# A second buffer for k, an earlier load of one batch's k, half a transpose on TensorE, and a new order on VectorE in a hand-scheduled attention and MLP kernel

## The chip, the cores and the metric

One core of one Trainium2 chip. The metric is the device time of one execution in microseconds (us). Before the change the median was 270.38 us over the first three runs (270.26 to 271.22).

In the profile, PE is TensorE, PEld its weight loads, DVE is VectorE, ACT is ScalarE, POOL is GpSimd, SP is SyncE and SPq its queue, from which most DMA transfers are issued. In a timeline each line is: start, length, engine, source line, operation, output<-inputs, shape, number of instructions; in brackets the idle time ahead of it and what ended that. Source lines of an experiment are shifted by one to three, as it adds lines to the tables at the top.

## The reference, cut to what matters

```python
# q, k, v: 8 batches x 8 heads x 576 x 64, float32
q_s = softmax(q, axis=-1)             # over the 64 features
k_s = softmax(k, axis=2)              # over the 576 positions
kv  = einsum('bhsd,bhse->bhde', k_s, v)
x   = einsum('bhsd,bhde->bhse', q_s, kv)      # -> 4608 tokens x 512
h   = x @ w_in                                # 512 -> 2048
out = (h * sigmoid(h)) @ w_out                # 2048 -> 512
```

## The kernel before

The tokens go through in nine chunks (0 to 8). Each has a first product (x with w_in, then silu on ScalarE) and a second product (with w_out). Chunks 3 to 8 do both products by a seven-product scheme (Winograd's form of Strassen) instead of eight; the chunks before lead into that: chunk 0 is all standard, chunk 1 has a standard first product and a seven-product second one, chunk 2 does half of its first product in each way. Beside that run the attention of the batches ahead: exps, row sums, normalisation, the transpose of q, kv, and the product of q with kv that makes the next chunk's input (called the input product here, or xt).

The kernel fixes the order of each engine's instructions itself: they stand in the order in which they were recorded. That order comes from tables of positions, one per chunk; all pieces are sorted by position and then recorded:

```python
def mid(b):                       # attention of batch b, placed in chunk b-1
    p = PLAN[b - 1]
    for i in range(4):            # two exps of q, two of k
        x, y = (("qt", "eq"), ("kt", "ek"))[i // 2]
        put(b - 1, p["ex"][i], exp, b, x, y, i % 2)
    for cc in range(2):
        put(b - 1, p["qs"][cc], qsum, b, cc)                       # DVE row sum
        put(b - 1, p["qn"][cc], qnorm, b, cc, ENG[p["qe"][cc]])    # DVE or POOL
        # ... vcast, kv, kvcopy (cut)
    # loads of the batch after, from SP's queue
    put(b - 1, p["lq"], load, b + 1, "qt", q)
    put(b - 1, p["lk"], load, b + 1, "kt", k)
    put(b - 1, p["lv"], load, b + 1, "vt", v)
    if "tt" in p:                 # part of the transpose on TensorE
        if len(p["th"]) == 1:
            put(b - 1, p["tp"], tr_dma, b, nc.sync, 1 - p["th"][0])
        # ... tr (nine transposes) and trc (copy from PSUM) (cut)
    else:
        put(b - 1, p["tp"], tr_dma, b, nc.sync)    # all of it by one DMA transfer
```

The buffers, and the copy (the *ring* is the set of six PSUM tiles that the first product fills in turn; s1, u2 and the like are the sums that turn the seven products into the result, XS those of the input):

```python
LDB = {"qt": 1, "kt": 1, "vt": 1}     # SBUF buffers of loaded q, k, v
PSB = {"ring": 6, "ops": 2}           # PSUM: tiles of the first product, banks of the second

def after(t, k):                      # what follows product k of chunk t's second product
    ...
    if k == 1:                        # s1: the first PSUM bank copied out
        if PLAN[t + 1]["m1"][0]:
            nc.vector.tensor_scalar_mul(out=new("s1"), in0=o, scalar1=c)
        else:
            nc.scalar.activation(out=new("s1"), in_=o, func=ACT.Copy, scale=c)
    elif k == 6:
        add(new("u2"), WP[t, "s1"])   # DVE, reads the other bank
```

The softmax here doesn't subtract the row's maximum and nothing guards it: scores larger than these inputs give would overflow.

Of the kernel before, what the change touches and what calls it, by code (L numbers as in the profile page):

```python
# [16 lines left out]
WARM = 1  # L17

PLAN = {
    0: {'y': [31.0, 33.0, 33.0, 33.5, 34.0, 34.5, 35.0, 35.0, 36.5, 37.0, 39.5, 41.5, 42.5, 44.5, 46.0, 47.0], 'ex': [31.7, 34.3, 38.3, 39.4], 'qs': [32, 36.0], 'qn': [36.5, 37.0], 'vs': [40.5, 37.5, 44.5, 44.0], 'ks': [45.0, 45.3], 'kc': [45.51, 46.81], 'lq': 33.5, 'tp': 38.0, 'ox': [47.1, 47.7], 'oc': [47.11, 47.71], 've': [2, 0, 1, 2], 'order': [(1, 0), (2, 0), (3, 1), (3, 0), (0, 0), (0, 1), (1, 1), (6, 0), (2, 1), (5, 0), (6, 1), (7, 1), (4, 0), (11, 0), (8, 1), (5, 1), (4, 1), (7, 0), (8, 0), (9, 0), (9, 1), (11, 1), (10, 1), (13, 1), (12, 1), (14, 0), (14, 1), (10, 0), (15, 0), (12, 0), (15, 1), (13, 0)], 'ke': [1, 0], 'oe': [0, 1], 'qe': [0, 0], 'pad': 16, 'th': [0, 1], 'tt': [42.5, 37.4, 43.0, 40.4], 'tc': [43.51, 40.5, 43.01, 42.5], 'te': [0, 2, 0, 0]},  # L20
    1: {'ex': [15.7, 17.22, 23.74, 21.26], 'qs': [17.5, 19.0], 'qn': [19.51, 19.1], 'vs': [25.0, 20.0], 'ks': [26.0, 21.5], 'kc': [26.51, 25.01], 'lq': 17.0, 'lk': 20.6, 'lv': 23.2, 'tp': 20.5, 'ox': [28.0, 28.5], 'oc': [29.01, 28.51], 've': [2, 2], 'pa': [11.4, 13.0, 11.5], 'pae': [0, 0, 0], 'ke': [1, 1], 'oe': [2, 1], 'std': 4, 'order': [], 'add': {}, 'act': {}, 's1': {0: 0, 1: 0, 2: 0, 3: 1}, 'sl': [1.5, 1.5, 3.0, 6.0, 5.0, 9.5, 6.5, 9.0, 10.0, 11.5, 12.5, 11.0, 14.5, 13.0, 15.0, 15.0], 'xs': [6.8, -21.4, -1.0, -4.5], 'xe': [0, 0, 1, 1], 'pad': 14, 'qe': [1, 0]},
    2: {'std': 2, 'order': [(3, 1), (3, 6), (2, 1), (2, 6), (3, 7), (3, 5), (2, 7), (3, 4), (2, 2), (2, 5), (3, 2), (2, 4), (2, 3), (3, 3)], 'y': [-13.0, -12.5, -11.0, -11.0, -11.0, -11.0, -10.0, -9.5, -8.0, -7.0, -3.5, -2.5, -2.0, -1.0], 'ex': [-1.207, -2.202, -1.08, 2.294], 'qs': [6.9, 1.4], 'qn': [11.91, 3.41], 'vs': [-1.58, 13.9], 'ks': [19.4, 19.9], 'kc': [19.41, 19.91], 'lq': 17.45, 'lk': 16.262, 'lv': 24.41, 'tp': 15.9, 'ox': [19.9, 20.4], 'oc': [19.91, 20.41], 'sl': [5.0, 5.5, 3.0, 4.0, 4.5, 7.5, 9.5, 10.0], 'add': {(3, 6): 9.55, (3, 3): 22.02, (3, 2): 16.02, (3, 1): 9.55, (2, 6): 11.55, (2, 2): 17.02, (3, 5): 13.55}, 'act': {(2, 3): 21.55, (3, 5): 17.02, (3, 3): 22.02, (2, 5): 19.02, (3, 4): 18.55, (2, 2): 16.02, (2, 1): 10.55, (2, 6): 15.02, (2, 4): 21.55, (3, 6): 9.55, (2, 7): 14.55}, 's1': {2: 0, 3: 1}, 'xs': [0.1, 2.1, 9.1, 2.6], 'pa': [19.95, 19.95, 20.45], 'ya': {5: -5.0, 4: -1.55, 2: -8.0, 7: -8.55, 3: -0.55}, 'm1': [0, 0], 'pb': [-14.9, -14.3, -14.2, -15.0, -10.5], 'xe': [0, 0, 0, 0], 'pae': [1, 1, 1], 'pbe': [0, 0, 0, 0, 0], 've': [1, 2], 'ke': [0, 1], 'oe': [1, 0], 'qe': [1, 0]},
}
STEADY = {'std': 0, 'order': [(0, 1), (0, 6), (0, 5), (0, 7), (0, 2), (1, 1), (0, 4), (1, 6), (0, 3), (2, 1), (1, 2), (1, 7), (1, 5), (2, 6), (1, 4), (1, 3), (2, 2), (2, 7), (2, 5), (2, 4), (3, 1), (3, 6), (2, 3), (3, 2), (3, 7), (3, 5), (3, 4), (3, 3)], 'y': [0.5, 1.5, 5.0, 6.0, 9.0, 9.5, 9.5, 12.5, 14.5, 18.0, 19.5, 22.5, 25.7, 28.402], 'ex': [3.798, 1.41, 3.92, 1.297], 'qs': [11.4, 6.9], 'qn': [12.41, 9.91], 'vs': [10.9, 12.92], 'ks': [19.4, 19.4], 'kc': [21.91, 20.41], 'lq': 8.95, 'lk': 23.9, 'lv': 24.41, 'tp': 17.4, 'ox': [23.4, 23.4], 'oc': [24.41, 26.41], 'sl': [], 'add': {(3, 6): 22.02, (0, 3): 8.02, (0, 2): 6.02, (0, 5): 5.02, (2, 2): 20.02, (1, 3): 15.55, (1, 4): 15.55, (2, 7): 17.55, (1, 2): 10.55, (0, 4): 8.02, (1, 1): 6.02, (2, 6): 14.55, (1, 6): 10.55, (3, 1): 20.55, (1, 7): 11.55, (3, 2): 24.02}, 'act': {(0, 2): 4.55, (0, 3): 10.02, (2, 5): 18.55, (0, 4): 9.02, (1, 5): 15.02, (3, 3): 27.404, (1, 3): 18.02, (0, 5): 5.02, (3, 4): 26.55, (1, 4): 17.02, (2, 4): 23.02, (2, 3): 23.02, (0, 6): 4.02, (1, 1): 8.02, (3, 6): 22.55, (0, 1): 2.55, (3, 5): 27.55, (2, 1): 13.02, (3, 2): 23.55, (3, 7): 27.02, (1, 7): 13.55, (2, 6): 15.02, (2, 7): 17.02, (1, 2): 12.55}, 's1': {0: 0, 1: 1, 2: 0, 3: 0}, 'xs': [0.296, 0.298, -0.227, 0.4], 'pa': [19.95, 27.407, 27.41], 'pb': [1.45, 1.96, 4.45, 4.46, 3.45], 'ya': {6: 8.0, 5: 18.5, 4: 22.95, 3: 28.852, 7: 14.5}, 'm1': [0, 0], 'xe': [0, 0, 1, 1], 'pae': [1, 1, 1], 'pbe': [0, 0, 1, 1, 1], 've': [1, 2], 'ke': [1, 1], 'oe': [0, 0], 'qe': [1, 1]}
for _t in range(3, 8):
    PLAN[_t] = STEADY
PLAN[8] = {'std': 0, 'order': [(0, 1), (0, 6), (0, 2), (0, 7), (1, 1), (0, 5), (0, 4), (0, 3), (1, 6), (1, 2), (1, 7), (1, 5), (1, 4), (2, 1), (1, 3), (2, 6), (2, 2), (2, 7), (2, 5), (3, 1), (2, 4), (2, 3), (3, 6), (3, 2), (3, 7), (3, 5), (3, 4), (3, 3)], 'y': [1.5, 2.0, 5.5, 8.5, 10.0, 11.0, 14.0, 15.0, 19.0, 22.0, 24.5, 25.8, 27.401, 27.406], 'sl': [], 'add': {(2, 7): 17.55, (3, 2): 24.02, (3, 7): 24.55, (3, 4): 26.55, (3, 1): 20.55, (2, 3): 22.55, (0, 2): 3.55, (0, 3): 8.02, (2, 4): 20.55, (1, 4): 13.55}, 'act': {(2, 1): 15.55, (3, 6): 24.02, (3, 4): 26.55, (2, 3): 24.55, (2, 4): 21.55, (1, 7): 14.02, (2, 6): 19.02, (0, 3): 10.02, (1, 5): 12.55, (0, 4): 8.02, (3, 5): 27.403, (1, 4): 15.02, (2, 7): 21.02, (3, 7): 25.55, (1, 6): 10.02, (1, 3): 15.55, (3, 2): 23.55, (2, 2): 19.02, (3, 1): 20.02, (0, 5): 7.55, (1, 1): 6.55, (2, 5): 20.02}, 's1': {0: 1, 1: 0, 2: 1, 3: 1}, 'xs': [-0.71, -0.208, -0.207, 1.4], 'pa': [24.45, 27.45, 29.429], 'pb': [0.793, 3.96, 12.45, 10.46, 11.45], 'ya': {6: 10.0, 4: 27.401, 7: 15.45, 2: 11.95}, 'm1': [0, 0], 'xe': [0, 0, 1, 0], 'pae': [1, 1, 1], 'pbe': [0, 1, 0, 1, 0]}
PLAN[9] = {'y': [0, 1, 2, 3, 4, 5, 6, 7, 8, 9, 10, 11, 12, 13], 'ya': {}, 'm1': [0, 0], 'pb': [-0.201, -0.2, -0.2, 1.9, 2.9], 'pbe': [0, 0, 0, 0, 0]}
TXAT = [(0, (1, -39.0, 0, 1)), (0, (1, -12.0, 1, 1)), (1, (1, -39.0, 0, 1)), (1, (1, 4.0, 1, 1)), (2, (1, 2.5, 0, 0)), (2, (1, -15.0, 1, 1)), (3, (1, -1.0, 0, 1)), (3, (2, -18.0, 1, 1))]
TWAT = [(1, -11.0, 0), (1, 4.0, 0), (1, 5.5, 1), (1, 13.0, 1), (1, 13.0, 0), (1, 20.0, 0), (0, 37.0, 0), (0, 40.5, 0)]  # L30
WORDER = ['w10', 'w11', 'w12', 'w13', 'w20', 'q', 'w21', 'w22', 'k', 'w23', 'v0', 'v1']
GATE = ('ek', 0)
HV = (1, 1.5, 1)
JS = 5
STD = 0
START = {'qn': (0, 0), 'h': [4, 3, 2, 1], 'v': 0, 't': (0, 0, 0, 2), 'x': 1, 'o': 0, 'w': 4}
# [2 lines left out]
def kernel(  # L39
# [57 lines left out]
    ctx.enter_context(tc.manual_schedule())  # L97

    st = [dict() for _ in range(B)]
    LDB = {"qt": 1, "kt": 1, "vt": 1}  # L100

    def load(b, name, src, ccs=None, eng=nc.sync, js=(0, J)):
        if name not in st[b]:
            st[b][name] = ld.tile([128, NG, J * D], FP32, name=name, bufs=LDB[name])
        x = src[b].rearrange("(g r) (p j) d -> g (r p) (j d)", r=2, j=J).rearrange("g x y -> x g y")
# [127 lines left out]
    def xtcopy(t, cc, dve=0):  # L233
        for i, (off, size) in enumerate(part[t]):
            o1 = XO.pop((t, cc, i), None)
            if o1 is None:
                continue
            for g in range(2):
                x = XT[t][:, 2 * cc + g, off:off + size]
                if g < dve:  # L240
                    nc.vector.tensor_copy(x, o1[g][:, 0:size])
                else:
                    nc.scalar.copy(out=x, in_=o1[g][:, 0:size])
# [332 lines left out]
    def load_w(name):  # L576
        if name[:2] == "w1":
            f = slice(*WCUT[int(name[2])])
            nc.gpsimd.dma_start(
                out=W1[:, :, f], in_=w_in[:, f].rearrange("(c p) f -> p c f", p=128)  # L580
            )
        elif name[:2] == "w2":
            i = int(name[2])
            nc.gpsimd.dma_start(
                out=W2[:, i * 4:(i + 1) * 4, :],
                in_=w_out[i * 512:(i + 1) * 512, :].rearrange("(fc p) o -> p fc o", p=128),
            )
        else:
            cc = int(name[1]) if len(name) > 1 else None
            load(1, name[0] + "t", {"q": q, "k": k, "v": v}[name[0]], cc, eng=nc.gpsimd)  # L590
# [18 lines left out]
    nc.gpsimd.tensor_copy(gate[:, 0:1], gx)  # L609
    for name in WORDER[:START["w"]]:  # L610
        load_w(name)
# [32 lines left out]
    xtcopy(0, 1, 1)  # L644
    for name in WORDER[SB["w"]:]:
        load_w(name)
# [9 lines left out]
    def put(t, pos, f, *args):  # L656
        todo.append((base[t] + pos, len(todo), f, args))
# [3 lines left out]
    def load_first(b):  # L661
        st[b]["qt"] = ld.tile([128, NG, J * D], FP32, name="qt", bufs=LDB["qt"])
        V.tensor_copy(st[b]["qt"][0:1, 0, 0:1], vaug[0:1, J - 1, D:E1])
        for x in (("qt", q), ("kt", k), ("vt", v)):
            load(b, *x)
# [33 lines left out]
    def xtpair(t):  # L699
        p = PLAN[t - 1]  # L700
        for cc in range(2):
            put(t - 1, p["ox"][cc], xt, t, cc)
            put(t - 1, p["oc"][cc], xtcopy, t, cc, p["oe"][cc])
# [19 lines left out]
    if STD == 1:  # L723
        put(*HV[:2], halve, ENG[HV[2]])
    for i, x in enumerate(PLAN[0]["y"]):
# [11 lines left out]
    for t in range(1, NCH):  # L737
        xtpair(t)
    for i, x in TXAT:
        put(*x[:2], vsum, i, *((0, HF // 2), (HF // 2, HF))[x[2]], ENG[x[3]])  # L740
    for i, x in enumerate(TWAT):
        put(*x[:2], wsum, i // 2, i % 2, ENG[x[2]])
# [42 lines left out]
```

## Time and profile before

| what | before |
|---|---|
| median of all four runs | 270.32 us (269.69 to 271.22) |
| profiled run | 269.08 us, span of the core 267.2 us |
| PE busy | 254.0 us of the span |
| chunk 1's second product starts | 60.69 us |
| chunk 2's first matmul | 76.50 us |
| chunk 2's first Winograd product | 85.63 us |
| input products of chunks 4 and 8 | 116.93 and 221.26 us |

The rows with a time are start times, and they are the best ruler here. A matmul's end is modelled, and a wait can hide in it; a start can't. I call the distance from 60.69 to 85.63, 24.94 us, the *lead-in*, and that from 116.93 to 221.26, 104.33 us, the *steady stretch*.

### The profile page before, as it was taken

To read this page: it belongs to the slowest core of one execution; us is meant where nothing else is said; L and a number is where in the kernel's file an instruction comes from. 1 tells how busy PE (TensorE), PEld (TensorE's weight loads), DVE (VectorE), ACT (ScalarE), POOL (GpSimd) and SP (SyncE) were. 2 spreads that over 40 slices of the span, in tenths; PEclk is the share of its full clock that TensorE was granted. 3 is DMA by queue.
4 is the path that set the end of the run, shared out by engine and by line. 5 is a ranking of instruction groups with operands and counts; after the bars stand their busy time and mean duration, and the time that the engine had idled before them with its cause. 6 is when DMAs were issued, how large, how long until landed. Compare 5 with 4: busy or idle time off the path is not lost.

```text
span 267.2 us, 6566 instructions
## 1 busy us (share of the span) xinstructions
PE 254.0 (95%) x2686; PEld 199.4 (75%) x2686; DVE 192.4 (72%) x332; ACT 187.3 (70%) x327; POOL 150.1 (56%) x94
## 2 busy tenths in 40 slices
PE   8889999998997999999999999999999999999993
PEld 3468645456844778888888888888888887888882
DVE  2930088757785989969986889688967678898842
ACT  5789964769649799878987798779875457454300
POOL 2655903941104959794978496859685546603500
PEclk9999999999999999999999999999999999999999
DMA  7999999910996895459655955592631102110334
GB/s 257 324 205 273 245 337 394 322 30 11 248 287 234 199 398 183 107 122 355 218 111 106 360 179 120 110 328 76 128 82 43 39 22 59 42 39 9 77 76 118
DMA packets 40717, 45.90 MB, mean 172 GB/s; under 512 B 16368, under 2 KB 28656, under 8 KB 40688
## 3 DMA queue, kind: packets, MB, share of 16 engines
q1 hardware_dynamic: 35392, 37.63, 47.0%
q0 software_dynamic: 5136, 7.73, 12.9%
q8 instruction: 21, 0.34, 0.5%
q10 hardware_dynamic: 160, 0.13, 0.2%
q14 instruction: 8, 0.07, 0.1%
HBM read 36.70 MB, written 9.44 MB: 173 GB/s over the span
## 4 chain that ended last, share of the span: by engine, by line
PE 65%; DMA 9%; DVE 9%; ACT 8%; SPq 5%; issue 3%; DVEq 0%; ACTq 0%
PE ops L450 26%; PE hps L349 20%; PE hps L256 10%; DMA kt<-in_k_dram 7%; PE ops L535 5%; SPq L524 4%; DVE u L367 2%; ACT eq L118 2%; ACT GT L286 2%; DVE zq L137 1%; PE kvps L183 1%; DMA qt<-in_q_dram 1%; ACT ek L118 1%; PE o L225 1%; SPq L159 1%
## 5 line engine op out<-in xcount | busy, mean ns | idle before, releaser
L450 PEld LDWEIGHTS <-GT 128*128 128x128 bf16 x512 | 49.6, 98 | 7.5 <-issue 1.2
L349 PEld LDWEIGHTS <-TX 128*128 128x128 bf16 x416 | 40.2, 98 | 8.5 <-issue 3.1
L349 PE MATMUL hps<-XS,TX 128*128 128x256 bf16 x312 | 43.1, 273 | 1.7 <-DVE u L367 0.9
L367 DVE SCALAR_TENSOR_TENSOR u<-hps,u 128x512 f32<-128x512 f32 x52 | 35.8, 688 | 10.8 <-PE hps L349 8.4
L367 DVE SCALAR_TENSOR_TENSOR u<-hps,s 128x512 f32<-128x512 f32 x52 | 35.5, 683 | 9.7 <-PE hps L349 9.4
L450 PEld LDWEIGHTS <-SW 128*128 128x128 bf16 x384 | 37.3, 98 | 4.9 <-DVE SW L407 0.4
L137 DVE TENSOR_REDUCE zq<-eq 128x18 f32<-128x1152 bf16 x16 | 21.5, 1347 | 23.9 <-ACT eq L118 23.9
L256 PE MATMUL hps<-XT,W 128*128 128x320 bf16 (+3 forms) x224 | 35.7, 318 | 2.8 <-ACT GT L286 1.7
L391 ACT ACTIVATE GT<-u 128x512 bf16<-128x512 f32 x52 | 32.2, 630 | 6.7 <-DVE u L367 6.7
L256 PEld LDWEIGHTS <-W 128*128 128x128 bf16 x224 | 21.7, 98 | 16.5 <-issue 3.9
L349 PEld LDWEIGHTS <-W 128*128 128x128 bf16 x312 | 30.4, 98 | 4.1 <-issue 0.4
L450 PE MATMUL ops<-W,GT 128*128 128x256 bf16 x256 | 31.7, 273 | 1.1 <-ACT s L480 1.1
L450 PE MATMUL ops<-TW,SW 128*128 128x256 bf16 x256 | 32.7, 273 | 0.0
L450 PE MATMUL ops<-TW,GT 128*128 128x256 bf16 x256 | 32.6, 273 | 0.0
L349 PE MATMUL hps<-XT,W 128*128 128x256 bf16 x208 | 30.4, 273 | 0.0
L405 POOL TENSOR_TENSOR SW<-GT 128x1024 bf16<-128x1024 bf16 x7 | 14.9, 2130 | 26.9 <-ACT GT L391 16.8
L411 POOL TENSOR_TENSOR SW<-GT,SW 128x1024 bf16<-128x1024 bf16 x11 | 23.6, 2148 | 9.2 <-DVE SW L407 9.2
L286 ACT ACTIVATE GT<-hps 128x192 bf16<-128x192 f32 (+4 forms) x72 | 25.0, 418 | 4.4 <-PE hps L256 3.1
L145 POOL TENSOR_TENSOR eq<-eq,rzq 128x1152 bf16<-128x1152 bf16 x10 | 21.3, 2127 | 9.5 <-DVE rzq L138 9.5
L118 ACT ACTIVATE ek<-kt 128x1152 bf16<-128x1152 f32 x16 | 18.3, 1158 | 10.4 <-DMA kt<-in_k_dram 10.4
L409 POOL TENSOR_TENSOR GT<-GT 128x1024 bf16<-128x1024 bf16 x12 | 25.6, 2131 | 0.0
L391 ACT ACTIVATE GT<-s 128x512 bf16<-128x512 f32 x26 | 16.5, 633 | 9.9 <-DVE s L367 9.9
(78 smaller groups left out, 396.5 us busy)
## 6 DMA issues: line engine op xcount, KB each, us to landing
qt<-in_q_dram SPq DMA_DIRECT2D x6, 1152.0 KB, 5.7
kt<-in_k_dram SPq DMA_DIRECT2D x6, 1152.0 KB, 6.5
vt<-in_v_dram SPq DMA_DIRECT2D x6, 1152.0 KB, 8.2
out_dram<-u SPq DMA_DIRECT2D x34, 64.0 KB, 3.4
W<-in_moe_w_in_dram POOLq DMA_DIRECT2D x4, 512.0 KB, 8.6
W<-in_moe_w_out_dram POOLq DMA_DIRECT2D x4, 512.0 KB, 18.9
out_dram<-u SPq DMA_DIRECT2D x14, 128.0 KB, 2.7
qt<-in_q_dram SPq DMA_DIRECT2D x2, 576.0 KB, 4.2
```

Source lines behind the costliest of these rows:

```text
L118: nc.scalar.activation(out=o, in_=jgd(st[b][src], cc)[:, js], func=ACT.Exp)
L137: nc.vector.reduce_sum(out=st[b]["zq"][:, cc, js], in_=e, axis=AX.X)
L145: eng.tensor_tensor(out=e, in0=e, in1=r[:, :, :, None].to_broadcast([128, n, 2, D]), op=ALU.mult)
L256: nc.tensor.matmul(out=hps[:, 0:size], lhsT=W1[:, c, fb * 128:(fb + 1) * 128], rhs=XT[t][:, c, off:off + size], start=(c == 0), stop=(c == ...
L286: nc.scalar.activation(out=y, in_=hps[:, h], func=ACT.Silu)
L349: nc.tensor.matmul(out=o[:, f, :], lhsT=l(c, 2 * g + f), rhs=r(c), start=bool(first and f == 0 and c == 0), stop=(c == HK - 1), skip_group ...
L367: nc.vector.scalar_tensor_tensor(out=out, in0=o, scalar=1.0, in1=x, op0=ALU.mult, op1=ALU.add)
L391: nc.scalar.activation(out=y, in_=MP[t, g, x], func=ACT.Silu)
L405: V.tensor_add(S1[:, f], quad(t, 0, f, 1), quad(t, 1, f, 1))
L409: V.tensor_sub(quad(t, 0, f, 1), quad(t, 0, f, 0), quad(t, 0, f, 1))
L411: V.tensor_sub(S4[:, f], quad(t, 1, f, 0), S2[:, f])
L450: nc.tensor.matmul(out=o, lhsT=l(f), rhs=r(f), start=bool(first and (own or a == 0) and f == 0), stop=(f == HF - 1), skip_group_check=True,)
```

## The change

Its intent: remove TensorE's waits in the lead-in. Batch 3's k is loaded earlier, into a second buffer. Half of batch 2's q is transposed by TensorE, so that less hangs on the DMA transfer. The copy of the first bank goes to VectorE, which gets a new order around it. Chunk 0 is reordered to suit, with the first half of v loaded ahead of the last quarter of w_out, and batch 2's q later.

The diff, cut to its core (the tables of chunks 0 to 2 are almost wholly new; only entries that the text uses are kept, `...` marks cuts):

```diff
 PLAN = {
-    0: {... 'lq': 33.5, ...}
+    0: {... 'lq': 39.0, ...}
-    1: {'ex': [15.7, 17.22, 23.74, 21.26], 'qs': [17.5, 19.0], 'qn': [19.51, 19.1], ... 'lk': 20.6, ... 'tp': 20.5, ... 'oe': [2, 1], ...}
+    1: {'ex': [16.7, 16.72, 22.24, 23.26], 'qs': [17.65, 17.9], 'qn': [19.1, 18.1], ... 'lk': 7.5, ... 'tp': 18.1, ... 'oe': [0, 2], ... 'th': [0], 'tt': [22.5, 21.1], 'tc': [23.51, 24.6], 'te': [2, 2]}
-    2: {... 'ex': [-1.207, -2.202, -1.08, 2.294], ... 'm1': [0, 0], ... 'qe': [1, 0]}
+    2: {... 'ex': [0.2, -0.79, -3.6, -4.09], ... 'm1': [1, 0], ... 'qe': [1, 1]}
 }
-TXAT = [(0, (1, -39.0, 0, 1)), (0, (1, -12.0, 1, 1)), ...]
+TXAT = [(0, (0, -5.5, 0, 0)), (0, (0, 20.0, 1, 1)), ...]
-WORDER = ['w10', ..., 'w22', 'k', 'w23', 'v0', 'v1']
+WORDER = ['w10', ..., 'w22', 'k', 'v0', 'w23', 'v1']
-    LDB = {"qt": 1, "kt": 1, "vt": 1}
+    LDB = {"qt": 1, "kt": 2, "vt": 1}
```

## The prediction

> **What bounds the kernel now.** I read the busy table first, then the busy time by stretches, then TensorE's instructions in order of time wherever it sat idle, and last what the engine named as releaser was doing just before.
>
> The first two lines of the page and the row of the idle tail:
>
> ```profile
> span 267.2 us, 6566 instructions
> PE 254.0 (95%) x2686; PEld 199.4 (75%) x2686; DVE 192.4 (72%) x332; ACT 187.3 (70%) x327; POOL 150.1 (56%) x94
> PEclk9999999999999999999999999999999999999999
> ```
>
> TensorE is busy 95% at full granted clock. Whatever leaves its work alone can win only what it idles, 267.2 - 254.0 = 13 us. The busy times by stretch (columns: stretch, its length, then busy us of PE, PEld, DVE, ACT, POOL) tell where that idle time is:
>
> ```profile
> 0.00:15.70 15.70, 12.75 (x140) 5.81 (x140) 10.01 (x23) 9.38 (x12) 7.86 (x17) 1.00 0.94 277
> ...
> 60.70:76.30 15.60, 14.32 (x201) 11.56 (x199) 11.67 (x20) 12.21 (x18) 2.12 (x1) 1.00 0.62 144
> 76.30:85.60 9.30, 7.21 (x32) 3.14 (x33) 6.97 (x12) 6.58 (x9) 2.15 (x2) 1.00 0.87 317
> 85.60:97.00 11.40, 10.60 (x163) 8.28 (x162) 9.36 (x20) 9.56 (x20) 9.10 (x6) 1.00 0.82 243
> 97.00:141.00 44.00, 44.00 (x544) 38.82 (x543) 38.03 (x66) 38.16 (x60) 35.19 (x20) 1.00 0.67 198
> ...
> 260.00:267.20 7.20, 2.93 (x27) 2.38 (x25) 1.54 (x3) 0.00 (x0) 0.00 (x0) 1.00 0.44 109
> ```
>
> The start (3.0 us idle) and the tail (4.3 us) are not touched by the change. From 97 us on, the idle time is near zero until the tail. What is left, about 4.2 us, lies between 60.7 and 97 us: chunk 1's second product, chunk 2's first. TensorE's instructions there, in order of time (start, length, what; in brackets the idle time and who ended it):
>
> ```profile
> 62.44 1.99 PE L450 MATMUL ops<-TW,SW 128*128 128x256 bf16 x16
> 65.50 1.91 PE L450 MATMUL ops<-W,GT 128*128 128x256 bf16 x16 [1.07 <-ACT s L480]
> ...
> 75.05 1.05 PE L450 MATMUL ops<-W,SW 128*128 128x256 bf16 x8
> 76.50 0.39 PE L256 MATMUL hps<-XT,W 128*128 128x512 bf16 x1 [0.40 <-DVE XT L241]
> 77.09 5.12 PE L256 MATMUL hps<-XT,W 128*128 128x512 bf16 x23 [0.20 <-DVE XT L241]
> 83.91 1.89 PE L256 MATMUL hps<-XT,W 128*128 128x512 bf16 x8 [1.70 <-ACT GT L286]
> ```
>
> Modelled matmul ends hide some waiting, so I go by starts. A group of sixteen takes 1.75 us (60.69 to 62.44), so the start at 65.50 is 1.31 late; 76.50 and 77.09 are .58 and .37 late; 23 matmuls at .2185 from 77.09 end at 82.12, so 83.91 is 1.79 late. With .28 for three changes to small matmuls, that is 4.33 us lost from 60.69 to 85.63. ScalarE's instructions in the same time show why:
>
> ```profile
> 61.45 1.28 ACT L118 ACT_TABLE_LOAD   x1
> 62.75 2.22 ACT L118 ACTIVATE eq<-qt 128x1152 bf16<-128x1152 f32 x2
> 64.87 0.58 ACT L480 ACTIVATE s<-ops 128x512 f32<-128x512 f32 x1
> ...
> 79.73 2.22 ACT L118 ACTIVATE ek<-kt 128x1152 bf16<-128x1152 f32 x2 [2.69 <-DMA kt<-in_k_dram]
> 81.97 1.28 ACT L286 ACT_TABLE_LOAD   x1
> ```
>
> The copy of the first bank stands behind a table load and two exps, and TensorE needs that bank again. Later ScalarE itself idles 2.69 us for batch 3's k, issued at 72.66 because the only k buffer was being read until then. The two exps and the table load come after it, so the first silu starts at 83.26, and the seventh tile finds all six PSUM buffers of the ring full.
>
> **What the Trainium skill says.** "Trainium Kernel Development and Optimization", section Best Practices: "Double-buffer for performance: Overlap DMA with compute". The 2.69 us above is the transfer that was not overlapped. "ScalarE: Activation LUTs", section What ACT_TABLE_LOAD costs, gives 1283 ns for the load and some 1380 ns of drain more for a switch. This trace has 1.28 us and the exp starts at 62.75, right at its end: no drain shows, and I use 1.28. "VectorE: DVE Perf Modes", section The three transpose paths, gives 390 ns for a 128x128 on TensorE. In this trace ten of them start at 43.08 and the next work at 43.63, so 55 ns each in a row; I use that. "SBUF — State Buffer", in the box on the "DVE blocks DMA" trap, says that VectorE in a fast mode can keep GpSimd from writing descriptors of its own DMAs. The change puts VectorE work into the time when GpSimd issues its last loads (17.8 to 23.6 us); no line before shows such a stall, as VectorE was idle then.
>
> **The change part by part.** The build order shows the same matmuls but for nine more transposes; the orders within chunk 0 change but not their sum. I take the start of chunk 1's second product at 60.69 as before; its own uncertainty is a rival below. The new chain, with durations of this trace:
>
> (a) Copy of the first bank on VectorE. It stands after two of the sums made from the last silu. These run 61.47 to 62.85, the copy (.68 from PSUM) ends 63.5, before the bank is wanted at 64.19. Removed: 1.31. Added: VectorE then does one sum (.65), batch 2's row sum (1.35, to 65.4) and a reciprocal, and only then u2 (.68), ending near 66.25. TensorE wants that second bank at 60.69 + 3 x 1.75 = 65.94. New stall: .35. Net -.96.
>
> (b) Nine transposes on TensorE: 9 x .055 = +.5. GpSimd's normalisation of that half ends at 65.7 + 2.1 = 67.8, before the transposes at about 69; the two PSUM copies go to ScalarE (.65 and .6, to about 71.2). The transfer that is left covers half the data and starts at 69.2 as before, so I estimate about 3 us of the 4.9 to landing; xt wants it near 74. No wait.
>
> (c) Chunk 2's input. Both halves of the product between kv and xt are now in one row and ScalarE copies two of the four blocks, VectorE two (before: one and three). Batch 3's k was issued near 54 us, when the stores of chunk 0 end, and lands by 61; so its exps run at 71.2 to 73.4, with no wait. ScalarE's block copies end near 75.05 and VectorE's 75.6. TensorE reaches this point at 60.69 + 1.75 x 4 + .35 + .87 + .5 + .42 + .87 + .42 + 1.75 + .87 + .57 + .87 + about .3 for changes of shape = 75.5, and waits .1 to .2 instead of .95. Net -.8.
>
> (d) The ring. ScalarE: two exps of q from about 75.3 to 77.6, table load to 78.9, silus each .5. The seventh tile is wanted at 75.7 + 24 x .2185 = 80.9; the silu which frees its bank ends 79.4. Each following tile is .87 apart and its silu .5, so they keep ahead. Removed: 1.79. So the first Winograd product of chunk 2 starts near 75.7 + 32 x .2185 = 82.7 with hand rounding, or 82.3 by the earlier sums; before 85.63. Sum by parts: -.96 + .5 - .8 - 1.79 = -3.05, and by start times -2.9 to -3.3.
>
> (e) From there to the steady part: 14 products, kv and xt, 9.0 us before (85.63 to 94.63) with about .8 of waits. After, VectorE's sums are again one step behind: I get waits of about .1, .2 and .25 around kv and .3 before the next chunk. Net 0. The two q halves are both on GpSimd (4.25), end near 83 to 85, and the transpose (about 5 to land) is wanted near 89.5: close, no wait or .4.
>
> (f) The sums of weights moved from GpSimd to VectorE run in its 18 us idle time (16.5 to 34.5): hidden. Everything from chunk 3 on has the same instructions in the same order, and TensorE full; the shift is kept to the end. Total: -3.1, so 267.3.
>
> **The rivals.** (1) The gain is taken back later: GpSimd's late transpose for chunk 3, or VectorE, becomes the wait near 89 to 95 us. VectorE is at 9.36 of 11.40 there. It would leave 1 to 2 us of gain: 268.5 to 269.3. (2) The loads in chunk 0. v now goes ahead of the last quarter of w_out, which I expect near 41 us by the spacing of landings (v's halves landed 41.8 and 44.2 before) and which TensorE wants at about 42.5; batch 2's q starts 3 us later (after one normalisation), which eases the queue. If it slips by 2 us, or descriptors are delayed by VectorE, TensorE and the second v cast stall .5 to 1: 268. (3) The second k buffer does nothing by itself and the ring stall only shrinks, because exps and table load still precede the silus. Against it: 1.5 us slack in (d). It would make 269. (4) More than predicted: every wait vanishes and other waits (.3 to .5 at 158.75, 185.19 and 226.42 us) shrink too: 4.7 us, 265.7.
>
> **Range and chances.** 2% is 5.4 us, more than the whole 4.2 us idle time in reach, so faster by over 2% is nearly excluded. Slower by 2% would need 8 us of new waiting, against the slack found. The spread of the runs before (270.26 to 271.22) adds some .3. I take 267.3, and 266.2 to 269.0.
>
> **What would show it.** Right: no 1.7 us wait for silu and no 2.7 us wait of ScalarE for k; that k load issued near 54 us; the copy on VectorE at about 63; a new wait of some .35 us for u2 before the fourth group; the first silu of chunk 2 near 79; the first Winograd product at 82 to 83; chunk 3 starting about 3 us earlier; span near 264. Wrong: a wait for w_out or v in chunk 0 over .5 us, a wait for the transposed q before xt of chunk 3, idle time after 97 us above 1.5 us, or the k load held up behind the output stores until it lands after 71.

## The result, and the profile after

| | before | after |
|---|---|---|
| median, four runs each | 270.32 us | 267.53 us (266.12 to 267.92) |
| profiled run | 269.08 us, span 267.2 | 267.45 us, span 265.6 |
| chunk 0's first matmul to chunk 1's second product | 44.98 us | 44.88 us |
| lead-in (to chunk 2's first Winograd product) | 24.94 us | 21.65 us |
| from there to chunk 3's first product | 9.00 us | 8.92 us |
| from there to chunk 4's input product | 22.30 us | 22.61 us |
| steady stretch | 104.33 us | 105.44 us |

The ratio of the runs is 0.9885, 95% interval 0.9839 to 0.9931: about 3.1 us, within 2%. A ratio here is the mean time of one kernel's runs over that of the other's of the same rounds, so it isn't quite the ratio of the medians. Executions over 1.5% slower than the fastest of the same kernel are left out of the means.

The top of the page after:

```profile
span 265.6 us, 6583 instructions
PE 253.7 (96%) x2695; PEld 200.2 (75%) x2695; DVE 197.0 (74%) x335; ACT 187.9 (71%) x326; POOL 148.2 (56%) x94
```

The busy times by stretch after, for the two stretches that lost most before (same columns as in the prediction; the last three are the granted clock, the DMA engines' busy share and GB/s):

```profile
60.70:76.30 15.60, 15.53 (x215) 12.69 (x214) 12.62 (x25) 14.10 (x17) 2.12 (x1) 1.00 0.64 160
76.30:85.60 9.30, 9.20 (x56) 5.24 (x54) 7.13 (x12) 8.27 (x14) 5.83 (x4) 1.00 0.77 239
```

TensorE is busy 24.73 of these 24.90 us; before it was 21.53. Its instructions there after:

```profile
61.01 1.91 PE L450 MATMUL ops<-W,GT 128*128 128x256 bf16 x16
62.76 1.99 PE L450 MATMUL ops<-TW,SW 128*128 128x256 bf16 x16
64.58 1.91 PE L450 MATMUL ops<-W,GT 128*128 128x256 bf16 x16
66.56 1.91 PE L450 MATMUL ops<-TW,GT 128*128 128x256 bf16 x16
...
69.18 0.67 PE L164 MATMUL qtps<-ident,eq 128*128 128x128 bf16 x9
...
74.31 0.63 PE L225 MATMUL o<-qT,kvn 64*64 64x128 bf16 x16
74.87 1.05 PE L450 MATMUL ops<-W,SW 128*128 128x256 bf16 x8
75.75 7.07 PE L256 MATMUL hps<-XT,W 128*128 128x512 bf16 x32
82.66 0.60 PE L349 MATMUL hps<-XT,W 128*128 128x256 bf16 x4
```

There is not one bracket left. The third group starts 1.82 us after the second, against 3.06 before. The fourth starts 1.98 after the third, where 1.75 is the pace: .23 of new wait, though no bracket says so. The 32 matmuls from 75.75 are unbroken, where before they came in three pieces. VectorE and then ScalarE in the same time:

```profile
63.12 0.68 DVE L478 TENSOR_SCALAR s<-ops 128x512 f32<-128x512 f32 x1
63.72 0.68 DVE L409 TENSOR_TENSOR GT<-GT 128x1024 bf16<-128x1024 bf16 x1
64.32 1.34 DVE L137 TENSOR_REDUCE zq<-eq 128x18 f32<-128x1152 bf16 x1
65.70 0.27 DVE L138 RECIPROCAL rzq<-zq 128x18 f32<-128x18 f32 x1
65.88 0.63 DVE L472 SCALAR_TENSOR_TENSOR u<-ops,s 128x512 f32<-128x512 f32 x1
```

```profile
71.78 2.22 ACT L118 ACTIVATE ek<-kt 128x1152 bf16<-128x1152 f32 x2 [0.43 <-ACT qT L172]
74.75 1.07 ACT L243 CAST XT<-o 128x512 bf16<-128x512 f32 x2 [0.75 <-PE o L225]
75.71 2.23 ACT L118 ACTIVATE eq<-qt 128x1152 bf16<-128x1152 f32 x2
77.96 1.28 ACT L286 ACT_TABLE_LOAD   x1
79.25 3.04 ACT L286 ACTIVATE GT<-hps 128x512 bf16<-128x512 f32 x6
```

The copy is at 63.12, and the sum u2 behind the row sum ends near 66.5, which is what the fourth group starts on. The k exps run at 71.78 without a wait for k, and the first silu is at 79.25 instead of 83.26.

From chunk 3 on, both traces have three waits alike: two of .32 us for VectorE's u (158.75 and 185.19 before) and one of .50 (226.42 before). TensorE's other waits there are these, first in the kernel before and then after:

```profile
96.37 0.60 PE L349 MATMUL hps<-XS,TX 128*128 128x256 bf16 x4 [0.26 <-DVE XS L306]
```

```profile
91.58 0.60 PE L349 MATMUL hps<-XT,W 128*128 128x256 bf16 x4 [0.45 <-DVE XT L241]
...
93.62 0.61 PE L349 MATMUL hps<-XS,TX 128*128 128x256 bf16 x4 [0.57 <-DVE XS L306]
...
179.86 1.91 PE L450 MATMUL ops<-W,GT 128*128 128x256 bf16 x16 [0.63 <-ACT s L480]
```

So of the 3.29 us won in the lead-in, this pair of traces gives .31 back in chunk 3 and 1.1 in the steady stretch; chunk 0's first matmul also stood .42 later (16.13 for 15.71). So the spans of the two profiled runs differ by only 1.6 us while the medians differ by 2.8: the kernel before's profiled run was itself 1.2 us faster than its median. The steady stretch has the same instructions in both kernels, so that 1.1 had to be looked into.

### The profile page after: what moved, and what is told of

Its sections match the earlier page's. It is cut to its first block, busy times and chain, and to the rows that moved or that the text cites.

```text
span 265.6 us, 6583 instructions
## 1 busy us (share of the span) xinstructions
PE 253.7 (96%) x2695; PEld 200.2 (75%) x2695; DVE 197.0 (74%) x335; ACT 187.9 (71%) x326; POOL 148.2 (56%) x94
## 4 chain that ended last, share of the span: by engine, by line
PE 74%; DVE 8%; DMA 8%; ACT 4%; issue 2%; SPq 2%; DVEq 0%; ACTq 0%
PE ops L450 28%; PE hps L349 23%; PE hps L256 13%; PE ops L535 5%; DMA kt<-in_k_dram 5%; DMA vt<-in_v_dram 3%; DVE u L367 3%; PE kvps L183 2%; DVE zq L137 2%; PE o L225 1%; SPq L524 1%; ACT XT L243 1%; ACT eq L118 1%; PE qtps L164 1%; DVE s L367 1%
## 5 line engine op out<-in xcount | busy, mean ns | idle before, releaser
L137 DVE TENSOR_REDUCE zq<-eq 128x18 f32<-128x1152 bf16 x16 | 21.5, 1342 | 12.6 <-ACT eq L118 12.6
L145 POOL TENSOR_TENSOR eq<-eq,rzq 128x1152 bf16<-128x1152 bf16 x11 | 23.6, 2148 | 9.4 <-DVE rzq L138 9.4
```

The source lines that it names most:

```text
L137: nc.vector.reduce_sum(out=st[b]["zq"][:, cc, js], in_=e, axis=AX.X)
L145: eng.tensor_tensor(out=e, in0=e, in1=r[:, :, :, None].to_broadcast([128, n, 2, D]), op=ALU.mult)
```

## The experiments

Each row gives start distances, as in the tables above, and the time. "k wait" is the longest wait of ScalarE for k in chunks 4 to 6. Times and ratios are against the kernel before of the same rounds, whose median was 270.15 to 270.82.

| run | chunk 0 to 1 | lead-in | steady stretch | k wait | median us | ratio |
|---|---|---|---|---|---|---|
| before | 44.98 | 24.94 | 104.33 | 1.89 | 270.32 | |
| after | 44.88 | 21.65 | 105.44 | 2.75 | 267.53 | 0.9885 |
| e1_early_k | 45.57 | 23.21 | 105.66 | 2.42 | 268.76 | 0.9922 |
| e2_buffer_only | 45.05 | 24.91 | 105.08 | 2.58 | 270.37 | 0.9991 |
| e3_copy_on_dve | 46.28 | 24.23 | 106.24 | 3.24 | 270.60 | 0.9996 |
| e4_copy_on_act | 44.88 | 22.65 | 105.63 | 2.48 | 268.00 | 0.9892 |
| e5_no_transposes (wrong result) | 44.88 | 21.70 | 104.53 | 2.08 | 267.06 | 0.9872 |
| e7_k_late | 44.88 | 22.72 | 104.97 | 2.23 | 268.17 | 0.9914 |
| e9_whole_transfer | 44.87 | 22.09 | 105.70 | 2.44 | 267.47 | 0.9887 |
| e8_three | 44.88 | 21.86 | 103.68 | 0 | 265.64 | 0.9815 |
| e10_steady_k_again | 44.88 | 21.65 | 103.75 | 0 | 265.56 | 0.9819 |
| e11_two_k_loads | 45.90 | 23.38 | 103.70 | 0 | 267.45 | 0.9886 |
| e12_one_buffer_steady | 46.05 | 24.68 | 104.13 | 0 | 269.33 | 0.9954 |

e6_steady_k stands in the text alone, as its profile is of an execution of 1485 us. My theory at the start was that of the prediction: the lead-in's gain is a sum of separate parts, about 1.8 for the k load, 1 for the copy, the rest small. The rivals were that the buffer alone or the copy alone does it, or that a later wait takes it back.

### The k load with its buffer, and the buffer alone

To the kernel before:

```diff
-    LDB = {"qt": 1, "kt": 1, "vt": 1}
+    LDB = {"qt": 1, "kt": 2, "vt": 1}
+PLAN[1]['lk'] = 7.5
```

> The kernel before with one part of the change alone: two k buffers, and batch 3's k loaded in chunk 1 instead of behind the transpose. Theory (three removed waits, each worth its own size): ScalarE's 2.7 us wait for k vanishes, the first silu of chunk 2 comes at about 80.5 instead of 83.3 us, the 1.7 us wait of TensorE for it vanishes, the waits before it stay; 1.8 us faster (ratio 0.993). Rival (the early k load does nothing unless ScalarE's exps are also moved ahead of the silus, as the exps and the table load still stand before them): a stall of over 1 us stays, ratio over 0.997.

Measured: 268.76 us, ratio 0.9922 (0.9885 to 0.9958); the lead-in is 1.73 us shorter. TensorE and ScalarE:

```profile
66.17 1.91 PE L451 MATMUL ops<-W,GT 128*128 128x256 bf16 x16 [1.07 <-ACT s L481]
...
77.89 6.85 PE L257 MATMUL hps<-XT,W 128*128 128x512 bf16 x30 [0.20 <-DVE XT L242]
```

```profile
78.01 2.21 ACT L119 ACTIVATE ek<-kt 128x1152 bf16<-128x1152 f32 x2
80.23 1.28 ACT L287 ACT_TABLE_LOAD   x1
```

The k exps have no bracket, the matmuls from 77.89 run through, and the wait for the copy at 66.17 is untouched. The second run has the buffer and not the position:

```diff
-    LDB = {"qt": 1, "kt": 1, "vt": 1}
+    LDB = {"qt": 1, "kt": 2, "vt": 1}
```

> The kernel before with two k buffers and nothing else moved. Theory as now read from the traces: the load of batch 3's k was held by its place in the issue queue, behind the transpose (issued at 72.7 us, the exps that free the buffer ended at 69.1), so the second buffer alone moves nothing: same time within 0.3 us, k still issued near 72.7 and ScalarE still waiting 2.7 us. Rival (my prediction's words: the one k buffer was still being read): issue some us earlier, most of 1.8 us gained.

Measured: 270.37 us, ratio 0.9991 (0.9961 to 1.0021): nothing. ScalarE still waits for k:

```profile
79.93 2.22 ACT L118 ACTIVATE ek<-kt 128x1152 bf16<-128x1152 f32 x2 [2.34 <-DMA kt<-in_k_dram]
```

SyncE's queue shows the cause, first in the kernel before and then with the buffer:

```profile
69.19 3.37 SPq L159 DMA_TRANSPOSE qT<-eq  x1
72.66 0.53 SPq L108 DMA_DIRECT2D kt<-in_k_dram  x1
```

```profile
69.41 3.42 SPq L159 DMA_TRANSPOSE qT<-eq  x1
72.93 0.53 SPq L108 DMA_DIRECT2D kt<-in_k_dram  x1
```

The load stands behind the issue of the transpose, which takes 3.4 us of the queue, with one buffer or with two. In the changed kernel the same load is issued at 53.74. The buffer only makes that place legal, as batch 2's k is still unread then; no run tried the early place with one buffer.

### The copy alone, and the change without the copy

To the kernel before, and below it to the changed kernel:

```diff
+PLAN[2]['m1'] = [1, 0]
```

> The kernel before with only the copy of the first bank of chunk 1's second product moved from ScalarE to VectorE. Theory: the wait at 65.5 us (1.31 us by starts) goes, and a new one of 0.3 to 0.5 us for u2 appears before the fourth group, which stands behind the row sum on VectorE; the fourth group starts 0.8 to 1 us earlier. But the silu of chunk 2 still waits for k, whose load is tied to the transpose and so to VectorE, not to TensorE: up to all of the gain is lost at the ring stall, which grows from 1.7 to some 2.5 us. So the time stays within 0.4 us. Rival (the waits add up independently): 0.9 us faster.

```diff
+PLAN[2]['m1'] = [0, 0]
```

> The changed kernel with only that copy moved back to ScalarE. Theory: TensorE's third group waits again until about 65.9 us (1.1 to 1.3 us), no wait for u2 after it; net 0.9 us slower than the changed kernel in the start of chunk 2's Winograd products, so 268.4, ratio to before 0.992. Rival: with k early there is 1.5 us of slack at the ring and the delay is hidden: same as the changed kernel, 0.9885.

Undone in the changed kernel, the copy brings its wait back and lengthens the lead-in by 1.00 us; the time is 268.00, ratio 0.9892, so the difference of .5 us to the changed kernel's 267.53 is within the scatter of the runs, and it is the trace that shows this part:

```profile
65.38 1.91 PE L451 MATMUL ops<-W,GT 128*128 128x256 bf16 x16 [1.07 <-ACT s L481]
```

Done alone in the kernel before, the wait goes, .71 us of the lead-in is kept, and the time shows no difference (270.60, ratio 0.9996, 0.9956 to 1.0036; a gain of .7 us lies within that interval). That is partly a miss: the ring's wait did not grow to the expected 2.5 us, it was 1.58. The .71 was eaten in two other places in that profiled run: the way from chunk 0 to chunk 1 took 46.28 instead of 44.98, and the steady stretch 106.24. No instruction of either place was edited. I took both for a scatter of this kernel that I had not seen, and both are taken up below.

### Half the transpose on TensorE

> The changed kernel with all of batch 2's q transposed by DMA again (no transposes on TensorE for it). Theory (step b of the prediction): TensorE saves 9 x 0.055 = 0.5 us, but the whole DMA transpose lands 4.9 us after its issue at 69.5, near 74.4, where chunk 2's input product wants it, and ScalarE's exps of batch 3's q wait for it too: from chunk 1's second product to the first Winograd product of chunk 2 between 0.5 us shorter and 0.5 us longer than the changed kernel's 21.65 us, and the same total time within 0.6 us. Rival (the transposes on TensorE are what frees the path): over 1 us longer.

```diff
+for _k in ('th', 'tt', 'tc', 'te'):
+    PLAN[1].pop(_k)
```

This run failed: its result is wrong, relative error 15.2. With the entries gone, the one transfer for the whole of q stands at position 18.1, ahead of the normalisation of one half at 19.1, so it moved that half before it was normalised. Its timing says little, as the transfer started too early. Mended, with one entry more:

```diff
+for _k in ('th', 'tt', 'tc', 'te'):
+    PLAN[1].pop(_k)
+PLAN[1]['tp'] = 19.2
```

> The changed kernel, but batch 2's q transposed whole by one DMA transfer, after both halves are normalised; nine TensorE transposes and two PSUM copies fewer. This mends the run before it that transposed one half too soon and gave a wrong result. Theory (the transposes cost TensorE what they spare it in waiting, so this part is worth about nothing in this place): the transfer is issued near 8.5 us after the start of chunk 1's second product and lands 4.9 later, the product between kv and xt for batch 2 starts 13.1 to 13.6 after it (13.3 in the changed kernel) with a wait of 0.2 to 0.6 for the transposed q, and the first Winograd product of chunk 2 is 21.5 to 22.0 after it (21.65 in the changed kernel); time within 0.5 us of the changed kernel. Rival (the transposes are what lets chunk 2 start early): the wait is 1 us or more, the distance 22.6 or more, time 1 us longer than the changed kernel's 267.5.

Measured: correct, 267.47 us, ratio 0.9887, the same time as the changed kernel. The lead-in is 22.09, .44 more. TensorE:

```profile
73.22 0.25 PE L228 MATMUL o<-qT,kvn 64*64 64x128 bf16 x4
74.21 0.58 PE L228 MATMUL o<-qT,kvn 64*64 64x384 bf16 x12 [0.74 <-DMA qT<-eq]
```

The input product comes early (12.80 us after the start of the lead-in; in the changed kernel 13.30) and then stands for the transfer till 13.79. In the kernel before, the input product came at 74.48 - 60.69 = 13.79 with no wait, as the transfer (issued at 69.19, 5.0 us) had landed at 74.2: the wait for the copy, 1.31 us, had covered it. So once that wait is gone, the transfer takes its place, and the nine transposes pay for themselves: .44 us in the lead-in, measured, that run time can't resolve. My expectation was nearer the truth than its rival, but its lead-in (21.5 to 22.0), its input product (13.1 to 13.6) and its wait (.2 to .6) were missed by a little.

### k late again in the changed kernel

```diff
-    LDB = {"qt": 1, "kt": 2, "vt": 1}
+    LDB = {"qt": 1, "kt": 1, "vt": 1}
+PLAN[1]['lk'] = 20.6
+PLAN[2]['ex'] = [0.2, -0.79, 0.3, 0.4]
```

> The changed kernel with one k buffer, batch 3's k loaded behind the transpose, and its exps after those of q. Theory: k is issued near 71.5 us and lands 77.5 to 78.5, its exps end near 80.5, the first silu starts near 82 instead of 79.3, TensorE waits 1 to 1.5 us at the seventh tile; 1.2 us slower than the changed kernel to the first Winograd product, ratio to before 0.993. Rival (the other parts alone remove the stall): within 0.4 us of the changed kernel.

Measured: 268.17 us, ratio 0.9914; the lead-in is 1.07 us longer, and the ring's wait is back, smaller:

```profile
81.44 1.89 PE L258 MATMUL hps<-XT,W 128*128 128x512 bf16 x8 [0.91 <-ACT GT L288]
```

k was here earlier than I had expected: the issue of the half transpose takes only 1.40 us of the queue, so k was issued at 70.46 and landed at 76.5. The k exps ran at 77.27, straight behind the q exps and without a wait for k, so this is the pure cost of their order: two exps (2.2 us) stand between the q exps and the table load. In the changed kernel they fill ScalarE's idle time at 71.8 instead, and that is only possible when k is there by then.

### k in the steady chunks

The trace after shows ScalarE in chunk 6 (first fence), where before it had a smaller wait in the same place (second fence):

```profile
177.11 1.16 ACT L118 ACTIVATE ek<-kt 128x1152 bf16<-128x1152 f32 x1 [2.75 <-DMA kt<-in_k_dram]
```

```profile
178.73 1.17 ACT L118 ACTIVATE ek<-kt 128x1152 bf16<-128x1152 f32 x1 [1.82 <-DMA kt<-in_k_dram]
```

Both kernels load k near the end of each steady chunk; after, this one was issued at 170.28 and landed 6.8 us later, 2.75 after ScalarE was ready for it. Behind the k exp stand an exp of q and then the copy s of that chunk's first bank, at 179.23, and this is the .63 us bracket at 179.86 above. If that is the cause of the long steady stretch, an earlier load must remove it. To the changed kernel:

```diff
+STEADY['lk'] = 8.96
```

> The changed kernel with k loaded earlier in the steady chunks too: right after q, ahead of the transpose and the output stores. Theory (the later chunks give back part of the gain because ScalarE waits 0.9 to 2.8 us for k, just in time): those waits of ScalarE go, TensorE's waits for its copy (0.63 us) and for u behind it go, the four steady chunks take 103.8 to 104.4 us in place of 105.44 (from the input product of chunk 4 to that of chunk 8); 1 to 1.5 us faster than the changed kernel, ratio to before 0.984. Rival (transfers only trade places: the transpose or v becomes late instead): same steady time, a wait for the transposed q of 0.5 us or more.

Measured: five of the six runs at 264.99 to 265.41 us, correct, ratio 0.9802 (0.9774 to 0.9831); the other took 1485.18 us, and the profile was taken of that one. So the same kernel ran again:

> The same kernel as the run that issued k early in every steady chunk, again, because one execution of it took 1485 us and the profile was taken of that one. Theory (steady chunks lose time because k lands just as ScalarE wants it; with the second buffer it can be issued some 9 us into the chunk before instead): correct, 265 to 266 us, no wait of ScalarE for k from chunk 3 on, and from the input product of chunk 4 to that of chunk 8 103.5 to 104.2 us (105.4 in the changed kernel). Rival (the gain there came from somewhere else, say from an easier start): the stretch stays at 104.8 or more. The long execution: if it is a property of this kernel, it comes again in some of these runs; I expect that it does not.

Measured: 265.56 us (264.96 to 265.86), ratio 0.9819 (0.979 to 0.9849), no long run among the six. SyncE's queue and ScalarE:

```profile
151.66 0.51 SPq L109 DMA_DIRECT2D kt<-in_k_dram  x1
```

```profile
173.39 1.16 ACT L119 ACTIVATE ek<-kt 128x1152 bf16<-128x1152 f32 x1
```

k is issued 21.7 us ahead of its exp, no bracket is left there, and the steady stretch is 103.75. The theory held. With the wait for k the two .32 us brackets of TensorE went too, here and in the three runs below with k early. This version beats both kernels, about 2 us under the changed one.

Two further edits were tried on top: the row sum of batch 2 behind u2, to remove the .23 us, and two of chunk 3's four input copies on VectorE instead of one:

```diff
+STEADY['lk'] = 8.96
+PLAN[1]['qs'][0] = 17.85
+PLAN[2]['oe'] = [1, 1]
```

> The steady k as above, and two small ones: VectorE makes u2 before batch 2's row sum, and takes two of the four input blocks of chunk 3 instead of one. Theory: the late start of the fourth group (0.23 us) and most of the waits of 0.45 and 0.57 us at the start of chunk 3 go: 0.3 to 0.8 us faster than the steady k alone, the fastest kernel of the study, ratio to before 0.981. Rival (the same engine does the same work a little later): the waits reappear within one chunk, time as with the steady k alone.

Measured: 265.64 us, ratio 0.9815: the gain of the k load and nothing more. The fourth group did start in step (1.74 us after the third), but the row sum was now late, and the transposes took the wait over (lead-in 21.86, no shorter); chunk 3's wait for XS stayed at .58:

```profile
69.07 0.68 PE L167 MATMUL qtps<-ident,eq 128*128 128x128 bf16 x9 [0.26 <-POOL eq L148]
...
93.52 0.61 PE L352 MATMUL hps<-XS,TX 128*128 128x256 bf16 x4 [0.58 <-DVE XS L309]
```

Then the two k loads alone, in the kernel before, with its second buffer:

```diff
-    LDB = {"qt": 1, "kt": 1, "vt": 1}
+    LDB = {"qt": 1, "kt": 2, "vt": 1}
+PLAN[1]['lk'] = 7.5
+STEADY['lk'] = 8.96
```

> The kernel before with only three numbers changed: two k buffers, batch 3's k loaded in chunk 1, and k loaded early in the steady chunks. Theory (the two k loads add up, and they are independent of the reordering): the distance from the start of chunk 1's second product to chunk 2's first Winograd product is 23.2 as with batch 3's k alone, the stretch from chunk 4's input product to chunk 8's is 103.5 to 104.3, time 266.5 to 267.3, as good as the whole change. Rival (the steady chunks gain only where chunk 2 is ordered anew, or the queue is then too full for the output stores): the stretch is 104.8 or more, time 268 or more.

Measured: 267.45 us, ratio 0.9886 (0.9855 to 0.9916); one of its six runs was slow (271.46). Lead-in 23.38 and steady stretch 103.70, both as the theory had them; the time is .15 above its range. So three numbers give as much as the whole change. The last run asked whether the steady part needs the second buffer, which my expectation for the steady runs had assumed. To the kernel before, with one buffer:

```diff
+STEADY['lk'] = 8.96
```

> The kernel before, with one k buffer, and one number changed: in the steady chunks (3 to 7) k is loaded after the ninth step of the chunk instead of near its end. By then both exps of the k in the buffer are done (they stand before the fourth step), so one buffer should be enough there; the text of an earlier expectation, which ascribed the steady gain to the second buffer, would be wrong. Theory (place in the issue order, not the buffer, is what counts in the steady chunks): no wait of ScalarE for k in chunks 4 to 6, stretch from chunk 4's input product to chunk 8's 103.5 to 104.2 us, everything before chunk 3 as in the kernel before (24.9 from the start of chunk 1's second product to chunk 2's first Winograd product), time 1.0 to 2.2 us less than before: 268.2 to 269.4. Rival (the buffer is needed: the issue waits for the exps and delays the stores and transposes behind it): stretch 104.8 or more, time 269.8 or more.

Measured: 269.33 us, ratio 0.9954 (0.9923 to 0.9985), steady stretch 104.13, no wait for k. It doesn't need the buffer: in the kernel before's trace the second k exp of a chunk ended at 157.1 and the next k was issued at 173.00, so the one buffer stood free for 16 us.

### What the first chunk hid

The column "chunk 0 to 1" was not looked for. With the old order of chunk 0 it was 44.98, 45.57, 45.05, 46.28, 45.90 and 46.05 us in six profiled runs, mean 45.64; with the new order it was 44.87 or 44.88 in seven of seven. ScalarE's wait for v there, in the kernel before, in the one-number variant of it (e12), and after:

```profile
44.22 0.69 ACT L127 CAST vaug<-vt 128x576 bf16<-128x576 f32 x1 [0.35 <-DMA vt<-in_v_dram]
```

```profile
45.23 0.69 ACT L128 CAST vaug<-vt 128x576 bf16<-128x576 f32 x1 [0.70 <-DMA vt<-in_v_dram]
```

```profile
44.47 0.68 ACT L127 CAST vaug<-vt 128x576 bf16<-128x576 f32 x1
```

The second half of batch 1's v lands just when it is wanted, in some runs 1 us later, and TensorE's kv with it: .96 us of wait in e12 and none in the kernel before's profiled run. With the new order that wait of TensorE is gone in every trace: v's second half lands at 43.13 to 44.22 us, with the old order at 44.20 to 45.44. Why it lands earlier is not shown. The new load order puts only v's first half ahead of the last quarter of w_out; the second half is still last, and is issued no earlier (23.84 to 24.72, against 23.60 to 24.06). A rival cause is batch 2's q, whose load is issued at 38.9 to 39.5 us instead of 36.2 to 36.4. No run undid either part alone.

## Why the prediction was right

The time came out at 267.53 for a predicted 267.3. By its steps:

**(a) The copy: right.** Predicted net -.96, with the copy at about 63 and u2 ending near 66.25. Measured: 1.00 by undoing it (.71 when done alone), copy at 63.12, u2 to 66.5. The new stall was .23 for .35.

**(b) The transposes: wrong sign, small.** Predicted +.5 with nothing saved, since the transfer looked harmless. But it was hidden by the wait that (a) removed; without the transposes it costs 1.0, so they gain .44. The term that was mis-sized is the wait that they spare. The half transfer did not land in the estimated 3 us either: 4.8 us in this trace, just in time at 74.4, and 3.3 to 4.6 in four others; the whole took 4.7 to 5.6 in seven.

**(c) Chunk 2's input: right.** Predicted start 75.5 to 75.7, with .1 to .2 of wait; measured 75.75, with none that shows, from a lead-in that started .32 later than assumed. No run undid this part alone.

**(d) The ring: right in size, wrong in its reason.** Predicted -1.79; measured -1.73 alone, first silu at 79.25 for 78.9 to 79.3. But the prediction said that the late issue at 72.66 came "because the only k buffer was being read until then". The buffer alone did nothing; the load stood in the queue behind the transpose's issue. The second half of rival 3 (exps and table load still precede the silus) is true as a mechanism: when the k exps stay behind the q exps, .91 us of wait comes back.

**The sum** was -2.9 to -3.3 for the lead-in; measured -3.29.

**(e) Between lead-in and steady part: nearly.** Predicted net 0. To chunk 3 it was -.08: of the waits forecast around kv none shows, and .45 for .3 stands before chunk 3. Then chunk 3's wait for XS grew from .26 to .57, a loss of .31. Both figures return in every trace: from chunk 3 to chunk 4's input product it is 22.6 us in all seven with the new order of chunks 0 to 2 and 22.3 in all six with the old. Rival 1 did not come in the form of GpSimd's late transpose, but the profile puts these two waits down to VectorE, its other form.

**(f) "Everything from chunk 3 on ... TensorE full; the shift is kept to the end": this is the step that failed, though the total hid it.** The steady stretch is not full. Two rows of the busy times before, which the prediction's excerpt leaves out, show it:

```profile
141.00:200.00 59.00, 58.22 (x689) 50.24 (x688) 47.78 (x83) 49.04 (x83) 45.08 (x25) 1.00 0.57 165
200.00:260.00 60.00, 59.50 (x547) 52.34 (x545) 46.87 (x75) 28.14 (x49) 25.65 (x13) 1.00 0.19 46
```

That is .78 and .50 us of idle time, called "near zero", and rival 4 names its brackets. The steady stretch took 104.3 to 106.2 us in the nine traces with k loaded late (means 105.3 with the old lead-in, 105.25 with the new), and 103.7 to 104.1 in the four with k loaded early (e8, e10, e11, e12). So few traces don't show that the change lengthens or shortens it; the pair of profiled runs happened to show 104.33 and 105.44. The kernel before's line of ScalarE waiting 1.8 us for k in the steady chunks was in its profile too, and I had passed over it.

**The start** was taken as before. From chunk 0's first matmul on it is .1 us better in this pair and .76 on average, with v's second half landing earlier: rival 2 had feared the opposite. Its sentence that v goes ahead of the last quarter of w_out holds for v's first half only.

With means instead of one pair, the parts sum to -.76 - 3.29 - .08 + .31 - .1 = -3.9 us, and the runs show 2.8 (medians) to 3.1 (means). I could not close the rest. The other stretches repeat from trace to trace to a few hundredths of a microsecond, so it must lie in the steady stretch, the way from chunk 0 to 1 or what is ahead of it, of which there are only four to seven traces each. That the total came within .3 us of the forecast is therefore in part luck: a gain of .76 that was not counted met a loss of .31 and this rest, neither of them foreseen.

## What to carry to other kernels

A second buffer only permits an earlier load; what brings the gain is the place in the issuing queue, so look there first, at what stands ahead of the late transfer. When a wait is removed, ask what it was covering: here a transfer landed in its shadow. And measure distances between start times over several traces before calling a stretch full, since small waits hide in modelled ends and a single pair of profiles can differ by more than the effect.

## What the Trainium skill lacked or had wrong

- "Trainium Kernel Development and Optimization", section Best Practices, advises to double-buffer. It lacks that the buffer alone can be worth nothing (ratio 0.9991) and that an earlier place in the queue can gain with a single buffer (0.9954).
- "ScalarE: Activation LUTs", section What ACT_TABLE_LOAD costs: the load is right (1.28 us), but the 1380 ns of drain that it adds don't show here: the silu starts at 79.25, and the load ran from 77.96 to 79.24.
- "VectorE: DVE Perf Modes", section The three transpose paths, gives 390 ns for a 128x128 on TensorE and 1309 ns by DMA. In a row, nine on TensorE took .60 us from start to the next start, 67 ns each; and the DMA transfer took 3.3 to 4.8 us for nine such blocks (five traces) and 4.7 to 5.6 for eighteen (seven), so neither figure can be multiplied by a count.
- "SBUF — State Buffer", section SBUF: two separate sides, in the box on the "DVE blocks DMA" trap: no such stall showed. Two of GpSimd's DMA issues overlap VectorE sums at 21.99 and 24.45 us after, and took .77 and .70 us; with VectorE idle before, they took .71 to .75. Whether those sums run in the mode that the box means, no run shows.
- "TensorE: Matmul & The Clock Gate", section Seeing it yourself, tells of a clock stuck at a quarter for over 50 us. Here one execution of 1485 us had TensorE slow from end to end (matmuls of 128x256 at 1046 ns mean for 273, TensorE busy 1473 us) with a recorded clock of 1.000. VectorE and ScalarE were busy 199.7 and 194.6 us, much as ever. It came once in twelve runs of that kernel. The page says to cross-check a throttle counter, which this record does not hold; the cause stays open.
